# A fused mixer kernel: the second MLP's tokens turned by transposing transfers instead of TensorE

## The chip, the cores and the metric

The kernel runs on one core of one Trainium2 chip, in one launch. The metric is the device time of that core in microseconds: from runs of the whole kernel, the median is given. The trace is of one execution, taken by the hardware profiler; its times are counted from the first instruction.

## The reference

Three layers follow each other over 4 batches of 768 tokens with 384 channels: a gated linear attention with a complex decay, a first MLP behind a low-rank mixing of the tokens, and a second MLP behind a two-dimensional Fourier transform. The change lies in the last, which computes

```python
X = np.fft.fft(x, axis=1)
X = np.fft.fft(X, axis=2)
mixed = np.real(X).astype(np.float32)
u = x + mixed
mu = np.mean(u, axis=-1, keepdims=True)
var = np.mean((u - mu) ** 2, axis=-1, keepdims=True)
un = (u - mu) / np.sqrt(var + 1e-06)
ch = np.maximum(un @ w_ch1, 0.0) @ w_ch2
return (u + ch).astype(np.float32)
```

`w_ch1` is 384 x 1536 and `w_ch2` is 1536 x 384. Products are kept at nearly float32 accuracy: each operand is split into a float16 part and a float16 rest, and three products of the parts are summed.

## The kernel before

The work of a batch is cut in two **groups** of 384 tokens, `(b, g)`. For the second MLP there are eight groups, (0,0) to (3,1). A group takes 12 steps `f`, one for each 128 hidden channels. A step has nine matmuls that make the hidden values (`first_product`, lines 192 to 198 with `mm3`, lines 105 to 107), ScalarE's `hh` (line 201) and VectorE's `hl` (line 204), the two float16 parts of the rectified hidden values, and nine matmuls that add them to three sums (lines 210, 211 and 224).

`first_product` needs the normalised tokens with **channels on partitions**, 384 tokens long, in two float16 parts. The tokens lie with tokens on partitions, so `make_un` (line 1446) normalises three tiles of 128 tokens on VectorE (line 1453, `un`), turns each 128x128 block with TensorE (line 1459, nine for a group, into a PSUM bank `nt`), and splits the bank: ScalarE makes the float16 part (line 1461), VectorE subtracts it from the bank to make the rest (line 1462).

While a group's matmuls run, the next group's tokens are made ready. The generator `moe_units` gives two **slots** a step, numbered `n` = 0 to 47 over the two groups of a batch, and `put` (line 1536) hands the yields of a generator to slots:

```python
put(make_un(b, 1), (16, 17, 18, 19, 21, 23))
...
put(make_un(after, 0), (40, 41, 42, 43, 45, 47))
```

An even slot's work stands ahead of that step's `hh` and `hl`, an odd slot's behind them. Slots of the first group also hold the Fourier transform of the next batch (`dft`, line 1268): its folds on VectorE, its float16 parts `eeh`, `eel`, `ooh`, `ool` (lines 1327 and 1335, in slots 13 and 14), its first products `ac` and `as` on TensorE (slots 15 and 17), the parts and squares of those (lines 1327, 1335, 1341), and behind them the rest, which ends in slot 35 with the factors that `make_un(after, 0)` needs. Slot 40 holds the loads of the batch after that (`dft_loads`, line 1258: five transfers on SP's queue, the gathers on POOL's). The stores of a finished group (line 1469) go out on SP's queue, too.

From the second phase on (line 1517) every engine and queue runs its instructions in the order in which the program names them; `in_order` (line 591) makes each depend on the one before it on its engine. An instruction that waits thus holds back all behind it on its engine.

Tiles come from rings: the ring `un` has four buffers of 1536 bytes a partition, used by `un` and by the folds of `dft`; a PSUM ring of three banks (`ms`) holds `nt`, `ac`, `as` and the later products of `dft`. A tile waits until all readers of the ring's buffer four (or three) tiles earlier are done. `raw_cc` and `raw_ss` hold the Fourier constants until they are split, in slots 15 to 18 of the last group of the first MLP, and are unused from then on.

Of the kernel before, what the change touches and what calls it, by code (L numbers as in the profile page):

```python
# [8 lines left out]
F16 = mybir.dt.float16  # L9
# [7 lines left out]
ALU = mybir.AluOpType  # L17
# [5 lines left out]
DM = H * D  # L23
# [20 lines left out]
def whole_of(ap):  # L44
    return ap if ap.dtype == F16 else f32(ap)
# [3 lines left out]
def mixer_kernel(ctx, tc, a_in, qk_in, v_in, u_in, v4_in, w_in, cc_in, ss_in, cb_in, sb_in, id_in, mask_in, rows_in, out):  # L49
    nc = tc.nc  # L50
    V, A, G, T = nc.vector, nc.scalar, nc.gpsimd, nc.tensor
# [12 lines left out]
    def bank(name, pool=None):  # L64
        pool = pool or pms
        return pool.tile([128, 512], F32, tag={id(pms): "ms", id(pacc): "acc", id(phid): "hid"}[id(pool)], name=name)
# [9 lines left out]
    def pair(name):  # L76
        if parts16[0]:
            return moe.tile([128, 2, 384], F16, tag="u", name=name, bufs=5)
        return pfl[0].tile([128, 2, 384], F32R, tag="u32", name=name, bufs=3)
# [65 lines left out]
    parts16 = [True]  # L145
# [29 lines left out]
    def check_w(mi, f, z):  # L175

        hi = wt[mi, f][:, 0, z * 384 : (z + 1) * 384]
        unread = ft(f"chk{mi}_{f}_{z}", [128, 384], BF16, tag="chk", bufs=1)
        at = stats[:, list(BOUNDS).index(("w1", "w2")[z]), mi * FB + f : mi * FB + f + 1]
        kept(V.scalar_tensor_tensor, out=unread, in0=hi, scalar=1.0, in1=hi, op0=ALU.mult, op1=ALU.mult, accum_out=at)  # L180
# [35 lines left out]
    def moe_units(todo):  # L216

        acc = {}
        late = []
        lows = []  # L220

        def low(mi, b, g, f, hl, t):
            last_step = f == FB - 1
            T.matmul(acc[t], hl[:, TSS[t]], wt[mi, f][:, 0, 384:], start=False, stop=last_step and mi == 1)  # L224
            if last_step:
                if mi == 0:
                    extra1(b, g, t, acc[t])
                (finish1, finish2)[mi](b, g, t, acc[t])

        def second(mi, b, g, f, hh, hl, very_last):  # L230
            if f == 0:
                acc.update(enumerate(sums(f"acc{mi}_{b}_{g}")))
            lows.append((mi, b, g, f, hl))
            if very_last:
                for args in lows[:-1]:
                    for t in range(3):
                        low(*args, t)
                del lows[:-1]
            for t in range(3):
                second_product(mi, f, acc, hh, t)  # L240
                if very_last:
                    low(*lows[0], t)
            while not very_last and len(lows) > (f < FB - 1 and parts16[0]):
                args = lows.pop(0)
                for t in range(3):
                    low(*args, t)

        for mi, b in todo:
            for g in range(2):
                for f in range(FB):  # L250
                    hp = first_product(mi, f, (uts, unT)[mi][b, g], f"hp{mi}_{b}_{g}_{f}")
                    yield mi, b, g, f, 0
                    hh, hl = (hidden(f"{x}{mi}_{b}_{g}_{f}", x) for x in ("hh", "hl"))
                    positive(hp, hh)
                    positive_low(hp, hh, hl)
                    yield mi, b, g, f, 1
                    for args in late:
                        second(*args, False)
                    late = [(mi, b, g, f, hh, hl)]
        second(*late[0], True)  # L260
# [163 lines left out]
    def make_ut(b, g):  # L424

        uts[b, g] = pieces = []

        def piece(k):
            xp = bank(f"xp{b}_{g}_{k}")[:, :384]
            tokens(xp, b, g, k)  # L430
            mixed(xp, b, g, k)
            u = pair(f"u{b}_{g}_{k}")
            if parts16[0]:
                A.activation(u[:, 0], xp, AF.Copy, scale=UP)
                V.scalar_tensor_tensor(out=u[:, 1], in0=xp, scalar=UP, in1=u[:, 0], op0=ALU.mult, op1=ALU.subtract)
            else:
                A.copy(u[:, 0], xp)
                V.tensor_tensor(u[:, 1], xp, f32(u[:, 0]), ALU.subtract)
            pieces.append(u)

        for k in range(3):
            piece(k)
            if k == 2 and g == 1 and parts16[0]:
                A.activation(zst[b], f32(zst[b]), AF.Copy, scale=UP * WP[0] * WP[1])
            yield
# [745 lines left out]
    u2 = {}  # L1191
# [3 lines left out]
    def ft(name, shape, dt=F32, tag=None, bufs=1):  # L1195
        return pfl[0].tile(list(shape), dt, tag=tag or name.split(".")[0], name=name.replace(".", "_"), bufs=bufs)
# [61 lines left out]
    def dft_loads(b):  # L1258
        lo, hi = ([ft(f"{x}.{b}_{i}", [128, DM], tag="lh", bufs=15 if parts16[0] else 6) for i in range(3)] for x in ("lo", "hi"))
        u2[b] = lo, hi  # L1260
        xs[b] = {}
        for i in range(3):
            nc.sync.dma_start(lo[i], x1d[b][i * 128 : (i + 1) * 128, :])
            G.indirect_dma_start(hi[i], None, x1d[b], bass.IndirectOffsetOnAxis(ap=fc["rows"][:, i : i + 1], axis=0))
            if i < (2 if parts16[0] else 1):
                xs[b][i] = others(b, i)
# [179 lines left out]
    def make_un(b, g):  # L1446

        mv, rs = rstd[b]
        unT[b, g] = pieces = []
        uns = []  # L1450
        for t in range(3):
            un = ft(f"un.{b}_{g}_{t}", [128, DM], tag="un", bufs=4 if parts16[0] else 3)
            V.tensor_scalar(un, u2[b][g][t], mv[:, 3 * g + t, 0:1], rs[:, 3 * g + t : 3 * g + t + 1], ALU.subtract, ALU.mult)
            uns.append(un)
            yield
        for k in range(3):
            ps = bank(f"nt{b}_{g}_{k}")[:, :384]
            for t in range(3):
                T.transpose(ps[:, t * 128 : (t + 1) * 128], uns[t][:, k * 128 : (k + 1) * 128], ident)
            u = pair(f"n{b}_{g}_{k}")  # L1460
            A.copy(u[:, 0], ps)
            V.tensor_tensor(u[:, 1], ps, whole_of(u[:, 0]), ALU.subtract)
            pieces.append(u)
            yield
# [36 lines left out]
    def verdict():  # L1501

        tests = [(i, test) for i, x in enumerate(BOUNDS.values()) for test in x]
        ok = ft("ok", [128, len(tests), B * NC], tag="un", bufs=4)
        for o, (i, (op, bound)) in enumerate(tests):
            V.tensor_scalar(ok[:, o], stats[:, i], bound, None, op)
        within = const("within", [128, 1])
        V.tensor_reduce(within, ok, mybir.AxisListType.XY, ALU.add)
        ps = bank("kept")[:1, :1]
        T.matmul(ps, within, one, start=True, stop=True)  # L1510
        broken = const("broken", [1, 1], I32)
        V.tensor_scalar(broken, ps, 128 * len(tests) * B * NC - 0.5, None, ALU.is_lt)
        return broken
# [16 lines left out]
    for mi, b, g, f, half in moe_units([(0, B - 1)] + [(1, b) for b in range(B)]):  # L1530
        n = 2 * (FB * g + f) + half
        if n == 0:
            after = b + 1 if mi else 0
            side = {}

            def put(gen, slots):
                for at in slots:
                    side.setdefault(at, []).append(lambda: next(gen, None))

            if mi == 0:  # L1540
                put((fn() for fn in conversions), (1, 1, 2, 2, 15, 16, 17, 18))
                put(dft(0), FIRST_STEPS)
                put(make_ut(b, 1), (19, 21, 23))
                put(make_un(0, 0), (41, 42, 43, 43, 45, 47))
            else:
                if after < B:
                    put(dft(after), STEPS)
                put(make_un(b, 1), (16, 17, 18, 19, 21, 23))
                if after < B:
                    put(make_un(after, 0), (40, 41, 42, 43, 45, 47))  # L1550
            if after + 1 < B:
                put((dft_loads(x) for x in [after + 1]), [40])
        for item in side.get(n, []):
            item()
        if mi and (b < 2 and n in (24, 36, 44, 46) or b == B - 1 and n < 40):
            check_w(*checks.pop(0))
        if (mi, b, n) == (1, B - 1, 42):
            broken = verdict()
# [207 lines left out]
```

## Time and profile before

| | |
|---|---|
| median of 3 runs | 864.04 us (861.32 to 870.68) |
| the profiled execution | 863.16 us, its span 861.4 us |
| second MLP's first matmul | at 544.1 us |
| PE busy over the span | 93% |
| DVE, ACT busy | 73%, 52% |
| granted TensorE clock | 0.997 of full speed |

Engines: PE is TensorE's matmuls, PEld its weight loads, DVE is VectorE, ACT ScalarE, SP the queue of the plain transfers. Matmuls are pipelined: each is listed with about 0.33 us, but they start some 0.16 us apart, so the time that one takes from its engine is read from the starts.

### The profile page before, as it was taken

The numbers are of one execution on the slowest core, as the hardware profiler recorded it, in microseconds if no ns is written. First come the engines' busy times: TensorE is split into PE (matmuls) and PEld (weight loads), VectorE is DVE, ScalarE is ACT, GpSimd is POOL, SyncE is SP. The second block draws the span as 40 slices with busy tenths as digits, with TensorE's granted clock in tenths as the row PEclk, the third lists the DMA queues.
The fourth block names the chain that finished last, engine by engine and source line by source line (L and its number), as shares of the span: only waits on it lengthen the run. The fifth ranks groups of instructions, "written<-read, shape, count | busy, mean of one in ns | idle before, by whom it ended". The sixth has DMA issues, their size and how long they took to land.

```text
span 861.4 us, 17279 instructions
## 1 busy us (share of the span) xinstructions
PE 799.0 (93%) x6947; PEld 542.1 (63%) x6947; DVE 627.7 (73%) x1304; ACT 450.6 (52%) x845; POOL 36.1 (4%) x79
## 2 busy tenths in 40 slices
PE   0298999999899999999999999999999999999996
PEld 0187755567766677666776665666666666666663
DVE  6989689998779977988965846657485657645652
ACT  7976598798868679758733342142224123311210
POOL 1001000010000000000003200001010100000000
PEclk9999999999999999999999999999999999999999
DMA  9539933588392594359386120103010300000000
GB/s 357 68 67 127 299 108 95 136 160 197 71 200 89 140 201 112 120 125 187 84 133 222 47 74 1 38 1 102 1 47 1 101 29 1 29 1 28 1 29 32
DMA packets 47353, 83.06 MB, mean 96 GB/s; under 512 B 5600, under 2 KB 36576, under 8 KB 47264
## 3 DMA queue, kind: packets, MB, share of 16 engines
q1 hardware_dynamic: 45984, 77.94, 37.6%
q0 software_dynamic: 1280, 3.93, 1.4%
q8 instruction: 56, 0.92, 0.5%
q14 instruction: 33, 0.27, 0.1%
HBM read 53.39 MB, written 9.44 MB: 73 GB/s over the span
## 4 chain that ended last, share of the span: by engine, by line
PE 75%; ACT 12%; DVE 6%; DMA 4%; issue 2%; SPq 1%; DVEq 0%; ACTq 0%
PE acc L210 10%; PE acc L211 10%; PE hp L105 10%; PE hp L107 10%; PE hp L106 10%; PE acc L224 7%; PE sc L325 4%; PE y L343 3%; PE acc L1083 3%; DMA QT<-QK 3%; ACT ain L101 2%; ACT L97 2%; PE g L343 1%; ACT hh L201 1%; PE z L385 1%
## 5 line engine op out<-in xcount | busy, mean ns | idle before, releaser
L201 ACT ACTIVATE hh<-hp 128x384 f16<-128x384 f32 x192 | 93.5, 489 | 303.5 <-PE hp L107 295.3
L204 DVE SCALAR_TENSOR_TENSOR hl<-hp,hh 128x384 f16<-128x384 f32 x192 | 105.6, 554 | 134.5 <-ACT hh L201 133.7
L210 PE MATMUL acc<-w,hh 128*128 128x384 f16 x576 | 187.7, 326 | 3.6 <-ACT hh L201 3.4
L211 PE MATMUL acc<-w,hh 128*128 128x384 f16 x576 | 187.3, 326 | 0.0
L105 PE MATMUL hp<-u,w 128*128 128x384 f16 x288 | 94.6, 328 | 0.1
L107 PE MATMUL hp<-u,w 128*128 128x384 f16 x288 | 94.5, 328 | 0.0
L106 PE MATMUL hp<-u,w 128*128 128x384 f16 x288 | 94.5, 328 | 0.0
L105 PE MATMUL hp<-n,w 128*128 128x384 f16 x288 | 93.9, 326 | 0.0
L107 PE MATMUL hp<-n,w 128*128 128x384 f16 x288 | 93.9, 326 | 0.0
L106 PE MATMUL hp<-n,w 128*128 128x384 f16 x288 | 93.9, 326 | 0.0
L210 PEld LDWEIGHTS <-hh 128*128 128x128 f16 x576 | 56.3, 98 | 40.4 <-ACT hh L201 6.6
L105 PEld LDWEIGHTS <-w 128*128 128x128 f16 x576 | 56.5, 98 | 37.8 <-issue 0.5
L107 PEld LDWEIGHTS <-w 128*128 128x128 f16 x576 | 56.5, 98 | 37.6 <-issue 0.5
L106 PEld LDWEIGHTS <-w 128*128 128x128 f16 x576 | 56.5, 98 | 36.8 <-issue 0.7
L224 PE MATMUL acc<-w,hl 128*128 128x384 f16 x360 | 77.5, 326 | 0.0
L211 PEld LDWEIGHTS <-hh 128*128 128x128 f16 x576 | 56.4, 98 | 33.1 <-issue 0.4
L325 PE MATMUL sc<-QT 96*128 96x128 f32 x384 | 50.0, 284 | 10.6 <-DMA QT<-QK 9.8
L325 PEld LDWEIGHTS sc<-QT 96*128 96x128 f32 x384 | 47.1, 197 | 13.0 <-issue 11.7
L332 PE MATMUL kp<-ident,QK 128*128 128x128 f32 x120 | 19.8, 292 | 33.6 <-DVE QK L309 31.3
L224 PEld LDWEIGHTS <-hl 128*128 128x128 f16 x360 | 35.2, 98 | 23.6
L1083 PE MATMUL acc<-w,hl 128*128 128x384 f16 x216 | 48.6, 327 | 1.4 <-DVE hl L204 1.4
L97 ACT ACT_TABLE_LOAD x33 | 42.3, 1283 | 1.3 <-PEq L1752 0.7
(264 smaller groups left out, 1414.4 us busy)
## 6 DMA issues: line engine op xcount, KB each, us to landing
QT<-QK SPq DMA_DIRECT2D x144, 129.0 KB, 6.9
stw<-in_w_dram SPq DMA_DIRECT2D x48, 384.0 KB, 5.3
ain<-in_a_dram SPq DMA_DIRECT2D x12, 768.0 KB, 7.0
qkin<-in_qk_dram SPq DMA_DIRECT2D x12, 768.0 KB, 6.9
x1d<-x SPq DMA_DIRECT2D x24, 192.0 KB, 3.4
vin<-in_v_dram SPq DMA_DIRECT2D x18, 192.0 KB, 3.4
lo<-x1d SPq DMA_DIRECT2D x12, 192.0 KB, 3.7
out_dram<-lo SPq DMA_DIRECT2D x12, 192.0 KB, 2.0
```

The source lines that it names most:

```text
L97: ordered(lambda: A.preload_act_table_set(name))
L105: T.matmul(o, ah, bh, start=start, stop=False, skip_group_check=skip)
L106: T.matmul(o, ah, bl, start=False, stop=False, skip_group_check=skip)
L107: T.matmul(o, al, bh, start=False, stop=stop, skip_group_check=skip)
L201: A.activation(hh, hp, AF.Relu)
L204: V.scalar_tensor_tensor(out=hl, in0=hp, scalar=0.0, in1=whole_of(hh), op0=ALU.max, op1=ALU.subtract)
L210: T.matmul(acc[t], hh[:, TSS[t]], w[:, 0, 384:], start=f == 0, stop=False)
L211: T.matmul(acc[t], hh[:, TSS[t]], w[:, 1, 384:], start=False, stop=False)
L224: T.matmul(acc[t], hl[:, TSS[t]], wt[mi, f][:, 0, 384:], start=False, stop=last_step and mi == 1)
L325: T.matmul(ps[:, h, :], q[:, 128:256], q[:, :128], start=True, stop=True)
L343: T.matmul(out[p, hsl], l(h)[:, p], r[:, hsl], start=h == 0 and o + done == 0, stop=h == 7 and o + rest == len(ops) - 1, skip_group_check= ...
L1083: T.matmul(accs[t], hls[n][:, TSS[t]], wt[0, every[n][2]][:, 0, 384:], start=False, stop=False)
```

## The change

For the seven groups other than (0,0), in the main path, `make_un` splits first and turns afterwards. Each of its three tiles of 128 tokens is normalised as before (`un`). Then ScalarE writes its float16 part and VectorE the rest into a tile `n16` with tokens on partitions, both now from SBUF, and **one transfer with a transpose**, issued on SP's queue, turns the whole tile of 128 x 768 float16 values into its place in `nt`, a tile with channels on partitions. `nt` lies in the buffers `raw_cc` (groups `g` = 0) and `raw_ss` (`g` = 1). `n16` shares the ring `un`. The nine transposes on TensorE and the three PSUM banks of a group go away. The six yields are given to other slots: 11 to 16 instead of 16 to 23, and 36 to 41 instead of 40 to 47. A yield of an odd place normalises, the next one splits and issues the transfer, in the order of the list.

```diff
         mv, rs = rstd[b]
         unT[b, g] = pieces = []
+        if parts16[0] and (b, g) != (0, 0):
+            nt = ft(f"nt.{b}_{g}", [128, 2, 3, 384], F16, tag=("raw_cc", "raw_ss")[g])
+            pieces.extend(nt[:, :, k] for k in range(3))
+            for t in range(3):
+                un = ft(f"un.{b}_{g}_{t}", [128, DM], tag="un", bufs=4)
+                V.tensor_scalar(un, u2[b][g][t], mv[:, 3 * g + t, 0:1], rs[:, 3 * g + t : 3 * g + t + 1], ALU.subtract, ALU.mult)
+                yield
+                n = ft(f"n16.{b}_{g}_{t}", [128, 2, DM], F16, tag="un", bufs=4)
+                A.copy(n[:, 0], un)
+                V.tensor_tensor(n[:, 1], un, n[:, 0], ALU.subtract)
+                to = nt.rearrange("d z k t -> d (z k) t")[:, :, t * 128 : (t + 1) * 128]
+                nc.sync.dma_start_transpose(out=to, in_=n.rearrange("t z d -> t (z d)"))
+                yield
+            return
         uns = []
...
-                put(make_un(b, 1), (16, 17, 18, 19, 21, 23))
+                put(make_un(b, 1), (11, 12, 13, 14, 15, 16))
                 if after < B:
-                    put(make_un(after, 0), (40, 41, 42, 43, 45, 47))
+                    put(make_un(after, 0), (36, 37, 38, 39, 40, 41))
```

## Rows read from the trace of the kernel before

**Rows 1.** The page: span; busy us, share of the span and instructions of each engine.

```profile
span 861.4 us, 17279 instructions
...
PE 799.0 (93%) x6947; PEld 542.1 (63%) x6947; DVE 627.7 (73%) x1304; ACT 450.6 (52%) x845; POOL 36.1 (4%) x79
```

**Rows 2.** Busy time by stretch: start:end, length, then each engine; PEclk, DMA share, GB/s.

```profile
544.10:861.40 317.30, 309.61 (x2079) 195.75 (x2077) 188.21 (x524) 79.65 (x183) 9.26 (x11) 1.00 0.09 30
586.80:623.50 36.70, 36.70 (x240) 22.76 (x238) 21.92 (x64) 7.43 (x17) 2.99 (x4) 1.00 0.19 60
623.50:665.70 42.20, 41.88 (x305) 27.60 (x304) 27.36 (x70) 14.82 (x35) 2.16 (x2) 1.00 0.08 24
```

**Rows 3.** Waits of TensorE from 544 us on: us in total, times, longest.

```profile
PE nt L1459 <- ACT as L1341: 0.8, 3, 0.3
```

**Rows 4.** Line 1459 from 544 us on: count, duration min/median/max, first and last start.

```profile
L1459 PE MATMUL nt<-ident,un x63: 272/273/329, 576.6 to 815.7; 128*128 128x128 f32 x63
```

**Rows 5.** TensorE in order of time: start, us, instruction and count (seven places).

```profile
610.79 0.33 PE L105 MATMUL hp<-n,w 128*128 128x384 f16 x1
...
613.71 0.33 PE L105 MATMUL hp<-n,w 128*128 128x384 f16 x1
...
615.18 0.49 PE L1459 MATMUL nt<-ident,un 128*128 128x128 f32 x3
615.50 0.33 PE L210 MATMUL acc<-w,hh 128*128 128x384 f16 x1
...
623.47 0.33 PE L105 MATMUL hp<-n,w 128*128 128x384 f16 x1
...
646.58 0.24 PE L107 MATMUL as<-ss,ool 128*97 128x192 f16 x1
...
665.69 0.33 PE L105 MATMUL hp<-n,w 128*128 128x384 f16 x1
...
817.25 0.33 PE L105 MATMUL hp<-n,w 128*128 128x384 f16 x1
```

**Rows 6.** Groups by line and shape, from 380 us on: count, busy us, mean ns, idle before.

```profile
L1462 DVE TENSOR_TENSOR n<-nt,n 128x384 f16<-128x384 f32 x24 | 13.1, 547 | 4.1 <-ACT n L1461 4.1
...
L1461 ACT CAST n<-nt 128x384 f16<-128x384 f32 x24 | 11.4, 474 | 4.3 <-PE nt L1459 4.3
...
L1279 DVE TENSOR_TENSOR xe<-lo,hi 128x384 f32<-128x384 f32 x8 | 4.3, 542 | 0.0
...
L1327 ACT ACTIVATE ooh<-oo 128x776 f16<-128x776 f32 x4 | 3.4, 843 | 0.0
```

**Rows 7.** VectorE in order of time, [idle before <-releaser] (two places).

```profile
612.97 0.56 DVE L204 SCALAR_TENSOR_TENSOR hl<-hp,hh 128x384 f16<-128x384 f32 x1 [1.98 <-ACT hh L201]
...
643.21 0.56 DVE L204 SCALAR_TENSOR_TENSOR hl<-hp,hh 128x384 f16<-128x384 f32 x1 [0.22 <-ACT hh L201]
643.95 0.97 DVE L1335 SCALAR_TENSOR_TENSOR eel<-ee,eeh 128x776 f16<-128x776 f32 x1 [0.18 <-ACT eeh L1327]
644.83 0.96 DVE L1335 SCALAR_TENSOR_TENSOR ool<-oo,ooh 128x776 f16<-128x776 f32 x1
```

**Rows 8.** ScalarE in order of time.

```profile
650.54 0.49 ACT L201 ACTIVATE hh<-hp 128x384 f16<-128x384 f32 x1 [2.23 <-PE hp L107]
```

**Rows 9.** Transfers, whole span: a queue's packets, MB, share; issues, KB each, us to landing.

```profile
q1 hardware_dynamic: 45984, 77.94, 37.6%
...
QT<-QK SPq DMA_DIRECT2D x144, 129.0 KB, 6.9
...
lo<-x1d SPq DMA_DIRECT2D x12, 192.0 KB, 3.7
out_dram<-lo SPq DMA_DIRECT2D x12, 192.0 KB, 2.0
```

**Rows 10.** SP's queue in order of time: start, us in issuing, line, count.

```profile
592.62 0.45 SPq L1263 DMA_DIRECT2D lo<-x1d  x1
...
594.61 0.38 SPq L1263 DMA_DIRECT2D lo<-x1d  x1
```

**Rows 11.** Line 318, QT<-QK: its landing times.

```profile
DMA to landing us min/median/max: 3.1/6.9/9.6
```

## The prediction, made before the changed kernel was run

> **What bounds the kernel now.** I read the page first: TensorE is busy 93% of the span [rows 1]. An average over two phases says little, so next the busy time by stretch. In the second MLP TensorE works 309.61 of 317.30 us, at a granted clock of 1.00; in a group without a Fourier transform beside it 36.70 of 36.70 us, in one with it 41.88 of 42.20, while VectorE has 21.92 and 27.36 us of work there, ScalarE 7.43 and 14.82 [rows 2]. The reader is to see that nothing but TensorE's own work sets the length of this phase. The list of TensorE's waits agrees: from 544 us on one kind is left, 0.8 us in three waits, and it is a transpose that waits [rows 3]. So a microsecond taken off TensorE there is a microsecond off the end, and one that another engine adds counts only where TensorE then has to wait.
>
> **What goes.** 63 transposes stand after 544 us, all of them in the seven groups changed [rows 4]. Their listed 273 ns is the length of one in the pipeline, not its price. That is read from the starts: three transposes begin at 615.18, the next matmul at 615.50, 0.32 to 0.33 us for three [rows 5]. 21 such triples are 6.9 us. With them goes the wait of 0.8 us [rows 3], since no `nt` asks for a PSUM bank. The most that can be won is 7.7 us: there is no other idle time of TensorE in these groups, and its clock is full.
>
> **What is exchanged.** A group has three casts and three subtractions before and after. From PSUM they take 474 and 547 ns; the nearest rows from SBUF are 542 ns for a VectorE operation of this size, and 843 ns for a ScalarE cast of twice the size, so about 0.42 to 0.47 us for ours [rows 6]. I take no difference; a gain of a few hundredths each would fall in idle time. The three `un` stay.
>
> **What is moved.** Ahead of group (b+1,0), slots 36 to 41, both engines are mostly idle (VectorE waits 1.98 us ahead of one `hl` [rows 7]): nothing. Ahead of (b,1), slots 11 to 16, the work now stands among the last folds and the splits of `dft`. Ahead of `ool` in VectorE's order come two `un` and one subtraction, at starts 0.47 us apart 1.41 us (`eel` and `ool` start 0.88 us apart at 0.97 each [rows 7], so 0.09 overlaps: 0.55 takes 0.46 to 0.47). VectorE's idle time there, 0.22 + 0.18 us, takes up part [rows 7]. `ool` ended at 645.79; TensorE first reads it at 646.58 [rows 5, 7]: 0.79 us of slack. 1.41 - 0.40 - 0.79 = 0.22 us late, in three groups (b = 0, 1, 2): 0.7 us. If no idle time can be used it is 0.62 us each, 1.9 in all; if the engine overlaps more, nothing. I take 0.7.
>
> **What is added: 21 transposing transfers** of 192 KB. The trace has none. From below, a plain transfer of that size lands in 2.0 us (stores) to 3.7 us (loads); the nearest row that goes from SBUF to SBUF on the same queue, `QT<-QK`, 129 KB a transfer by the profile's count, has a median of 6.9 us and at most 9.6 in a stretch where the queue is crowded [rows 9, 11]. Cut in rows of 128 values (256 bytes) a transfer has 768 packets; the queue's mean packet cost 37.6% x 16 x 861.4 / 45,984 = 0.113 us for a mean of 1.7 KB, so by packets 768 x 0.113 / 16 = 5.4 us at most, and by bytes (77.94 MB in 37.6% of 861.4 us is 241 GB/s) 0.8 us. In this phase the queue is nearly empty (DMA share 0.09 [rows 2]), so I go by the bytes and the quiet 192 KB rows: 1 to 3 us of the queue, 2 to 5 us to landing, with no gain to be had below that, since the bytes have to move.
>
> What hides them: a step takes 613.71 - 610.79 = 2.92 us [rows 5]. Ahead of (1,0) the split of tile 2 stands behind the `hl` at 612.97, and both take 0.47 us from start to start [rows 7]; so the three transfers go out near 608.1, 611.1 and 614.0. The first product that reads them was at 623.47 and comes 1.0 us earlier without the three triples [rows 5]: 8.5 us of cover for the last. Ahead of (1,1) it is longer: tile 0's split stands ahead of the `hl` at 643.21 and, with one `un` and one subtraction more, its transfer goes out near 644.0, the last near 650; the reader, at 665.69 before, comes 1.3 us earlier (the triples and a wait), at 664.4 [rows 3, 5, 7]. Ahead of (3,1), without a transform, the first goes out six steps ahead of the reader: the reader at 817.25 - 1.0 = 816.2, the transfer at 798.7 [rows 5]. Three things are queued. **On SP's queue** the five loads of slot 40 stand between the second and the third transfer. Before, they went out from 592.62 on, long ahead of their slot, since nothing held them [rows 10]; now they wait for tile 1's split, to 611. Their readers are the folds of the next batch, after 623.5, and the batch takes 594.61 + 3.7 - 592.62 = 5.7 us, so they land by 617. The third transfer then stands behind them, and lands by 619 to 622. In time, with 0.5 us or more to spare. Stores wait for nothing new. **POOL's queue** is not moved past. **In the ring `un`** the third `n16` takes the first one's buffer, so ScalarE's third cast waits until the first transfer has landed, and `hh` and the square of `ac` stand behind it. That square frees the bank of the next `as`; ScalarE had 2.23 us idle ahead of that `hh` at 650.54, and the square stands right behind it [rows 8]. With a cast of 0.47 the first transfer may land as late as 650.1: 6.1 us after it was issued. At 2 to 5 us nothing is lost.
>
> **Sum:** 6.9 + 0.8 - 0.7 = 7.0 us off the profiled execution's 863.16 gives 856.2. That execution stands 0.9 us below the median of the runs; on the median, 864.04 - 7.0 = **857.0**.
>
> On the price of a turned block the Trainium skill has two figures. "VectorE: DVE Perf Modes", section "The three transpose paths", gives 1309 ns for a 128x128 block by the DMA crossbar, and the rules of that page advise TensorE wherever PSUM can take the result, which speaks against this change; six such blocks one after the other are, as an estimate, 7.9 us a transfer, and the sum would be about 900 us. "DMA: Bandwidth & Descriptors", section "Latency and other measured facts", gives 261 GB/s, as an estimate 0.75 us, which leaves the sum as it is. No row of this trace tells which holds.
>
> **The rivals.**
> *Crowding:* VectorE and ScalarE run late ahead of (b,1), and TensorE waits for `eel`, `ool` or for a bank. For it: VectorE is almost without gaps there, and a wait of 0.2 us is already forecast. Against: ScalarE is free, and later slots are emptier by the work moved out of them. If each of the three groups loses 1 to 2 us, the gain is 7.7 - 3 to 7.7 - 6: 859 to 862, say 860.5.
> *Slower:* the transfers run one after the other on SP's queue, each as long as the nearest SBUF-to-SBUF row, 6.9 us. They would land at 608.1 + 20.7 = 628.8 against a reader at 622.5: TensorE stands 6.3 us, ahead of (1,0), (2,0) and (3,0), 18.9 us. Ahead of (3,1), with no transform beside it, 798.7 + 20.7 against 816.2: 3.2 us. Ahead of the other (b,1) only the wait in the ring counts, 644.0 + 6.9 against 650.1: 0.8 us, three times. 24.5 us against 7.0 won: about 881. At 9.6 us each the same working gives 14.4 x 3 + 11.3 + 8.4 x 3 = 80 us, 937. It decides from (622.5 - 608.1) / 3 = 4.8 us a transfer on. For it: the nearest row, and that the values are turned. Against: that row is from a crowded stretch, and 241 GB/s by bytes. The skill's 1309 ns belongs to this rival.
> *The edit does less than it says:* if TensorE's starts close up by less than the triples' 0.33 us, because another wait fills it, there is no change, 864. TensorE without gaps on both sides of each triple speaks against it.
>
> **How the numbers follow.** The forecast has a chance of 0.63 (its own range 854 to 860, by the runs' scatter and the 0.7 us), crowding 0.12, the slow transfers 0.21, no effect 0.04. A measurement of this kernel tells about 1% from no change, 8.6 us: faster is below 855.4, slower above 872.7. Even the full 7.7 us stays short of that, so faster by over 1% comes only from the scatter of the runs (861.32 to 870.68): 0.17. Within 1% takes the rest of the forecast, crowding and no effect: 0.61. Slower 0.22. The range 853.5 to 882 leaves out the far half of the slow transfers, and a little scatter below.
>
> **What would show it.** Right: from 544 us on no transpose on TensorE; groups of 35.6 us without a transform and some 41 us with one; the transfers landing in under 5 us; no wait of TensorE for `nt`; `as` with waits of a few tenths. Wrong: a wait of the first product of a group for a transfer; ScalarE's cast waiting for one ahead of `hh`; loads that land behind the folds; or TensorE waits for `eel` and `ool` of over 0.6 us a group.

## The result, and the profile after

The changed kernel takes **856.0 us** (median of 14 runs, 854.33 to 859.34) against 863.87 us (14 runs): ratio 0.9906, 95% interval 0.9884 to 0.9929. Forecast were 857.0 us and a ratio within 1% of no change, on the faster side. Two single executions, 1698 us with the kernel before and 2124 us with all eight groups turned by transfers, are far off the rest: the medians below hold them, the ratios leave them out.

The head of the page and its line on DMA packets, changed kernel, and behind them the same line of the kernel before:

```profile
span 853.8 us, 17228 instructions
...
PE 791.8 (93%) x6884; PEld 534.8 (63%) x6884; DVE 627.7 (74%) x1304; ACT 451.1 (53%) x845; POOL 36.0 (4%) x79
...
DMA packets 64153, 87.19 MB, mean 102 GB/s; under 512 B 22400, under 2 KB 53376, under 8 KB 64064
...
DMA packets 47353, 83.06 MB, mean 96 GB/s; under 512 B 5600, under 2 KB 36576, under 8 KB 47264
```

TensorE has 63 instructions less than in [rows 1], VectorE and ScalarE as many as before. Now the busy time by stretch: the whole second MLP, group (0,1) and group (1,0), the stretches of [rows 2]:

```profile
544.80:853.80 309.00, 302.34 (x2017) 188.31 (x2014) 188.04 (x524) 80.19 (x183) 9.26 (x11) 0.99 0.17 44
586.20:621.90 35.70, 35.70 (x231) 21.70 (x229) 21.90 (x64) 7.51 (x17) 3.00 (x4) 1.00 0.31 78
621.90:662.70 40.80, 40.73 (x295) 26.51 (x294) 27.21 (x70) 14.78 (x35) 2.19 (x2) 1.00 0.15 40
```

The second MLP goes from 317.3 to 309.0 us, 8.3 less. The span falls by 7.6 only, since this execution's first phase, which the change does not touch, was 0.7 us longer. Groups without a transform fall by 1.0 us, those with one by 1.4, and TensorE is as full as before.

TensorE's waits from 535 us on, in place of [rows 3]:

```profile
PE nt L1473 <- DVE un L1467: 1.4, 1, 1.4
```

That one belongs to group (0,0), which is turned as before. No first product waits for a transfer. The transfers by their line: SP's time in issuing (min/median/max, first and last start), and the times to landing:

```profile
L1461 SPq DMA_TRANSPOSE nt<-n x21: 1210/1222/2057, 565.7 to 799.7; - x21
...
DMA to landing us min/median/max: 2.7/2.7/2.8
```

This trace holds the landing of six of the 21 transfers, none of them behind other transfers on the queue. A second trace of the same kernel (the changed kernel run again, below) holds all 21:

```profile
DMA to landing us min/median/max: 2.7/2.7/4.6
```

There 18 land in 2.7 to 2.9 us and one in 3.5; the two that stand behind five loads, ahead of (1,0) and (2,0), land in 4.6 and 3.6 us. Packets under 512 bytes rose from 5600 to 22,400, 800 a transfer: 768 rows of 256 bytes (128 float16 values) make up its 192 KB; what the other 32 are is not shown. SP's queue ahead of (1,0), where the loads stand between the second and third transfer (start, us in issuing):

```profile
607.61 4.14 SPq L1461 DMA_TRANSPOSE nt<-n  x2
611.79 0.57 SPq L1263 DMA_DIRECT2D lo<-x1d  x1
...
613.83 0.43 SPq L1263 DMA_DIRECT2D lo<-x1d  x1
614.36 1.22 SPq L1461 DMA_TRANSPOSE nt<-n  x1
```

The third goes out at 614.36 and its reader begins at 621.9. In the second trace it goes out at 623.6, lands at 628.2, and its reader begins at 631.1: 2.9 us to spare.

### The profile page after: what moved, and what is told of

Same layout as the page of the kernel before. It is cut to its first block, busy times and chain, and to the rows that moved or that the text cites. A ratio compares the mean times of both kernels' runs of the same rounds, so it can differ in the third digit from the quotient of the medians.

```text
span 853.8 us, 17228 instructions
## 1 busy us (share of the span) xinstructions
PE 791.8 (93%) x6884; PEld 534.8 (63%) x6884; DVE 627.7 (74%) x1304; ACT 451.1 (53%) x845; POOL 36.0 (4%) x79
## 2 busy tenths in 40 slices
DMA packets 64153, 87.19 MB, mean 102 GB/s; under 512 B 22400, under 2 KB 53376, under 8 KB 64064
## 4 chain that ended last, share of the span: by engine, by line
PE 74%; ACT 10%; DMA 6%; DVE 6%; SPq 2%; issue 1%; DVEq 0%; ACTq 0%
PE acc L210 10%; PE acc L211 10%; PE hp L105 10%; PE hp L107 10%; PE hp L106 10%; PE acc L224 7%; PE sc L325 4%; PE y L343 3%; DMA QT<-QK 3%; PE acc L1083 3%; ACT ain L101 2%; ACT L97 2%; PE g L343 2%; PE warm L609 1%; PE kp L332 1%
## 5 line engine op out<-in xcount | busy, mean ns | idle before, releaser
L105 PE MATMUL hp<-nt,w 128*128 128x384 f16 x252 | 82.2, 326 | 0.0
L106 PE MATMUL hp<-nt,w 128*128 128x384 f16 x252 | 82.2, 326 | 0.0
L107 PE MATMUL hp<-nt,w 128*128 128x384 f16 x252 | 82.2, 326 | 0.0
L325 PEld LDWEIGHTS sc<-QT 96*128 96x128 f32 x384 | 47.1, 197 | 12.8 <-issue 11.6
```

The lines of the kernel that those rows point to most:

```text
L105: T.matmul(o, ah, bh, start=start, stop=False, skip_group_check=skip)
L106: T.matmul(o, ah, bl, start=False, stop=False, skip_group_check=skip)
L107: T.matmul(o, al, bh, start=False, stop=stop, skip_group_check=skip)
L325: T.matmul(ps[:, h, :], q[:, 128:256], q[:, :128], start=True, stop=True)
```

## The experiments

Nine runs, each beside runs of the kernel before on the same chip. The first phase varies from execution to execution, by several microseconds (its end lies between 541 and 554 us in the profiles below, with the same instructions up to its last group), so each run is also judged by the length of its second MLP, from its first product to the end of the span, which repeats to 0.2 us (309.0 and 308.9 in two traces of the changed kernel, 309.1 and 308.9 in two with all eight groups).

**The slots alone.** The transposes stay on TensorE; the pieces lie in the two constant buffers.

```diff
+        nt = ft(..., [128, 2, 3, 384], F16, tag=("raw_cc", "raw_ss")[g]) if ... (b, g) != (0, 0) else None
-            u = pair(f"n{b}_{g}_{k}")
+            u = pair(f"n{b}_{g}_{k}") if nt is None else nt[:, :, k]
-                put(make_un(b, 1), (16, 17, 18, 19, 21, 23))
+                put(make_un(b, 1), (11, 12, 13, 14, 15, 16))
-                    put(make_un(after, 0), (40, 41, 42, 43, 45, 47))
+                    put(make_un(after, 0), (36, 37, 38, 39, 40, 41))
```

> The kernel before with the moved slots alone: TensorE still turns the blocks, the pieces lie in the two unused constant buffers, as in the change (the old ring of five can't hold a third piece that early). My theory: the time is TensorE's own work, so no change but for the 0.8 us of waits for a bank: ratio to before 0.998 to 1.003 (862 to 866 us), with 63 transposes at 0.33 us a triple still there. Rival: a part of the 8 us comes from the earlier slots and the other buffers, then 856 to 861 us (ratio 0.991 to 0.997).

Measured: 867.59 us, ratio 1.0064 (1.0042 to 1.0086): slower than either theory said. Its second MLP and TensorE's waits there:

```profile
541.80:861.30 319.50, 309.18 (x2079) 195.42 (x2077) 188.09 (x524) 79.26 (x183) 9.26 (x11) 0.99 0.09 30
```

```profile
PE ac L105 <- DVE nt L1463: 3.5, 3, 1.2
```

2.2 us longer than before: the 0.8 us of waits ahead of `nt` are gone, but in the three groups with a transform `ac` now asks for a bank of the ring that `nt` still holds, and waits up to 1.2 us. The early slots win nothing by themselves. The medians differ by 5.3 us (867.59 against 862.25 beside it). The other 3 us are not in this trace, whose execution took 863.06 us and whose first phase, 541.8 us, is no longer than the 544.1 before; where the other executions lost them is not shown.

**Each transpose twice.**

```diff
-            for t in range(3):
+            for t in [*range(3)] * (1 if (b, g) == (0, 0) else 2):
                 T.transpose(ps[:, t * 128 : (t + 1) * 128], uns[t][:, k * 128 : (k + 1) * 128], ident)
```

> The kernel before with each of the 63 transposes done twice into the same bank, nothing else changed. My theory: a triple costs 0.33 us of a TensorE without gaps, so 21 more triples cost 6.9 us: 870.8 us, ratio 1.008 (1.006 to 1.010). Rival: a transpose's listed 273 ns is its price, then 17 us more (ratio 1.020); or part of it hides in waits, then under 4 us (ratio below 1.005).

Measured: 872.04 us, ratio 1.0095 (1.0065 to 1.0126), and in the trace:

```profile
548.30:872.60 324.30, 316.49 (x2143) 202.69 (x2140) 189.36 (x524) 80.87 (x183) 9.23 (x11) 0.99 0.09 29
```

324.3 - 317.3 = 7.0 us for 21 more triples, 0.33 us each, with no new wait. This is the price of the transposes, shown by itself: the starts give it, the listed duration does not.

**The transfers at the old slots.**

```diff
-                put(make_un(b, 1), (11, 12, 13, 14, 15, 16))
+                put(make_un(b, 1), (16, 17, 18, 19, 21, 23))
-                    put(make_un(after, 0), (36, 37, 38, 39, 40, 41))
+                    put(make_un(after, 0), (40, 41, 42, 43, 45, 47))
```

> The changed kernel with the slots of before (16 to 23 and 40 to 47): the last transfer of a group goes out next to its reader. My theory: it lands 2.7 us after its issue, and the splits stand behind the last hl (and, ahead of (1,1), (2,1), (3,1), behind the sums of the transform), so the first product waits about 5 us ahead of (1,1) and (2,1) and (0,1), and 2 to 3 us ahead of (1,0), (2,0), (3,0), (3,1): 20 to 26 us over the changed kernel, 876 to 882 us, slower than before (ratio 1.014 to 1.021). Rival: the transfers are so short that their place does not matter, then 856 to 860 us.

Measured: 891.06 us, ratio 1.0336 (1.0306 to 1.0366). TensorE's waits from 530 us on, and the first of them by stretch (the wait, then three pieces of what follows):

```profile
PE hp L105 <- DMA nt<-n: 24.7, 7, 4.2
```

```profile
586.40:590.60 4.20, 0.04 (x1) 0.00 (x0) 2.31 (x9) 0.00 (x0) 0.00 (x0) 0.96 0.24 47
590.70:592.00 1.30, 1.30 (x5) 0.61 (x6) 0.00 (x0) 0.00 (x0) 0.00 (x0) 0.50 0.00 0
592.00:593.00 1.00, 1.00 (x5) 0.47 (x4) 0.00 (x0) 0.00 (x0) 0.00 (x0) 0.50 0.00 0
593.50:596.00 2.50, 2.50 (x25) 1.78 (x24) 1.69 (x6) 0.71 (x2) 0.00 (x0) 0.96 0.00 0
```

The waits are 24.7 us, as expected. But the second MLP takes 343.3 us, 34.3 more than in the changed kernel:

```profile
544.90:888.20 343.30, 311.56 (x2016) 191.19 (x2014) 188.42 (x524) 79.73 (x183) 9.13 (x11) 0.97 0.15 40
```

After the first wait the granted clock is 0.50, the 1.2 GHz level: matmuls start 0.32 us apart instead of 0.16.

```profile
590.64 0.48 PE L105 MATMUL hp<-nt,w 128*128 128x384 f16 x1 [4.20 <-DMA nt<-n]
590.92 0.52 PE L106 MATMUL hp<-nt,w 128*128 128x384 f16 x1
591.24 0.52 PE L107 MATMUL hp<-nt,w 128*128 128x384 f16 x1
```

So a late transfer can cost its lateness and more: 9.6 us went beside the 24.7, which I had left out, and 9.2 of them are TensorE's busy time grown for the same matmuls (311.56 against 302.34 us). Not every wait did this. Over the 5 us behind each of the seven, the mean granted clock was 0.66 to 0.69 five times and 1.00 twice, behind 3.05 us ahead of (2,0) and 2.94 us ahead of (3,1). Two waits of nearly the same length, 3.02 us ahead of (3,0) and 3.05 ahead of (2,0), show both:

```profile
804.00:809.00 5.00, 4.98 (x21) 2.61 (x22) 1.05 (x4) 0.49 (x1) 0.00 (x0) 0.66 0.00 0
718.30:723.30 5.00, 4.99 (x31) 3.04 (x32) 2.75 (x6) 0.49 (x1) 0.00 (x0) 1.00 0.02 5
```

No run separates what makes the difference.

**All eight groups by transfers**, run twice.

```diff
-        if parts16[0] and (b, g) != (0, 0):
+        if parts16[0]:
...
-                put(make_un(0, 0), (41, 42, 43, 43, 45, 47))
+                put(make_un(0, 0), (41, 41, 42, 43, 43, 44))
```

The buffer `raw_cc` is free by then: in the trace of the kernel before its constants are split by 487.4 us, in the group ahead of the last group of the first MLP, which begins at 503.7, and not in that last group.

> The changed kernel with the first group (0,0) turned by transfers too, its yields in slots 41, 41, 42, 43, 43, 44 of the last group of the first MLP. My theory: three triples (1.0 us) and TensorE's wait of 1.4 us for the third un go away, and the last transfer goes out some 5 us ahead of its reader and lands in 2.7: 2 to 2.4 us faster than the changed kernel, about 853.7 us, ratio to before 0.988. Rival: the first group has too little cover, TensorE waits 1 to 3 us for the transfer, and nothing is won (856 to 858).

Measured: 854.61 us, ratio 0.9895 (0.9867 to 0.9923). Against 0.9906 for the change that is too close to tell, so both were run again beside each other.

> The changed kernel itself, beside the next run on the same chip, so that the two can be compared directly. Theory: ratio to before 0.9906 as measured (0.988 to 0.993), no wait of TensorE for nt from a transfer. Rival for the small size: scatter of the first phase, then a ratio outside 0.988 to 0.993.

> All eight groups turned by transfers (the kernel of the run with the first group, again), beside the changed kernel. Theory: the last group of the first MLP is 2.6 us shorter (37.7 instead of 40.3), so 2 to 3 us faster than the changed kernel: ratio to before 0.986 to 0.989, with the second MLP at 309 us as in the changed kernel. Rival: within scatter of the changed kernel (0.990 to 0.992).

Measured: the changed kernel 856.86 us, ratio 0.9903 (0.9871 to 0.9936); all eight 853.61 us, ratio 0.987 (0.9831 to 0.9908). The intervals overlap, so the medians alone do not tell the two apart; the traces do. The last group of the first MLP and the second MLP, first in the changed kernel, then with all eight:

```profile
513.80:554.10 40.30, 38.90 (x272) 24.34 (x271) 22.97 (x64) 10.84 (x26) 0.00 (x0) 1.00 0.12 40
554.10:863.00 308.90, 302.31 (x2016) 188.11 (x2014) 188.00 (x524) 80.17 (x183) 9.26 (x11) 0.99 0.17 44
```

```profile
503.00:540.70 37.70, 37.70 (x263) 23.28 (x262) 23.07 (x64) 11.04 (x26) 0.00 (x0) 1.00 0.22 58
540.70:849.60 308.90, 302.30 (x2016) 188.08 (x2014) 187.99 (x524) 80.18 (x183) 9.13 (x11) 0.99 0.17 44
```

The group is 2.6 us shorter (three triples, 1.0, and the wait, 1.4, make up most of it), the second MLP the same. The first run of this kernel has the group at 37.7 us too, and every other trace here has it at 40.3. The rest of the difference between the two spans, 863.0 and 849.6, lies ahead of this group, where the two kernels are the same. This is the fastest version found; it beats the change by 2.6 us in this group and by 3 us in the medians.

**One block a transfer**, six transfers for one.

```diff
-                nc.sync.dma_start_transpose(out=to, in_=n.rearrange("t z d -> t (z d)"))
+                x = n.rearrange("t z d -> t (z d)")
+                for i in range(6):
+                    nc.sync.dma_start_transpose(out=to[:, i], in_=x[:, i * 128 : (i + 1) * 128])
```

> The changed kernel with each transfer cut into its six 128x128 blocks, six transfers for one, the same bytes. In the changed kernel a transfer occupies SP for 1.22 us and lands 2.7 us after its issue; a plain one occupies it 0.43. My theory: the 1.22 us is 0.4 fixed and the rest by blocks, so a block alone takes about 0.54 us of SP and 18 take 9.7 us; ahead of (1,0) and (2,0), with the five loads between, the last lands at the reader, and the kernel is 0 to 3 us over the changed one (856 to 859 us). Rival: nearly all of the 1.22 us is fixed, then 18 x 1.2 = 21.6 us a group, the last lands 6 to 9 us behind its reader ahead of three groups and 2 to 6 ahead of the others, and the kernel is 25 to 60 us slower, the half clock after each wait included.

Measured: 903.19 us, ratio 1.0498 (1.0436 to 1.056). My theory fell, the rival held. The transfers by their line, and TensorE's waits:

```profile
L1463 SPq DMA_TRANSPOSE nt<-n x126: 1100/1230/2090, 563.2 to 853.8; - x126
...
DMA to landing us min/median/max: 2.3/2.3/3.6
```

```profile
PE hp L106 <- DMA nt<-n: 17.7, 14, 3.6
PE hp L105 <- DMA nt<-n: 16.3, 3, 6.6
```

A block alone occupies SP for 1.23 us, six in one transfer for 1.22: the time is the transfer's, not the block's. Eighteen take 22 us of SP and can't keep up. 34.0 us of waits, and 356.2 - 309.0 = 47.2 us more in the second MLP:

```profile
543.40:899.60 356.20, 313.98 (x2016) 189.70 (x2014) 188.41 (x524) 80.28 (x183) 9.00 (x11) 0.95 0.14 38
```

Of the other 13.2 us, 11.6 are TensorE's busy time grown for the same matmuls (313.98 against 302.34), at a mean granted clock of 0.95: again the lower clock behind waits. Another 0.7 is a wait for VectorE.

**Four slots later.**

```diff
-                put(make_un(b, 1), (11, 12, 13, 14, 15, 16))
+                put(make_un(b, 1), (15, 16, 17, 18, 19, 20))
-                    put(make_un(after, 0), (36, 37, 38, 39, 40, 41))
+                    put(make_un(after, 0), (40, 41, 42, 43, 44, 45))
```

> The changed kernel with all its slots four later (15 to 20 and 40 to 45): two steps, 5.85 us, off the cover. My theory: the last transfer ahead of (1,0), (2,0), (3,0) goes out about 2.8 us ahead of its reader and lands in 2.7, so it is just in time: waits of TensorE for nt of under 1 us in all, and 855 to 858 us. Rival: the cover was needed (other traffic, late splits), then waits of 1 us and more a group and over 862 us.

Measured: 854.89 us, ratio 0.9907 (0.9873 to 0.994).

```profile
PE hp L105 <- DMA nt<-n: 0.5, 3, 0.2
```

```profile
611.72 7.12 SPq L1461 DMA_TRANSPOSE nt<-n  x3
...
543.10:853.20 310.10, 302.84 (x2017) 188.09 (x2014) 188.61 (x524) 79.70 (x183) 9.29 (x11) 0.99 0.16 44
```

Three waits of 0.2 us: ahead of (1,0) the last transfer goes out at 617.6, 2.9 us ahead of its reader at 620.5, and the cover is used up. The second MLP is 1.1 us longer than in the changed kernel, 0.5 of it in these waits. The edit changes one thing more: slot 40, which holds the five loads, is now that of the first yield and no longer of the fifth, so the loads go out ahead of all three transfers (from 590.3 on) and not between them. In the changed kernel the third transfer ahead of (1,0) has 7.5 us of cover and lands 4.6 us behind its issue in the second trace, so 2.9 us are to spare there, and not 5.85.

**Each transfer twice.**

```diff
-                nc.sync.dma_start_transpose(out=to, in_=n.rearrange("t z d -> t (z d)"))
+                for _ in range(2):
+                    nc.sync.dma_start_transpose(out=to, in_=n.rearrange("t z d -> t (z d)"))
```

> The changed kernel with each transfer issued twice, the second behind the first's landing, since it writes the same place. My theory: transfers cost nothing as long as the last lands ahead of its reader. A tile then takes SP about 5 us; ahead of (1,0) and (2,0), with the loads between, the last lands some 2 us late, elsewhere in time: 2 to 6 us over the changed kernel, 858 to 862 us, all of it in TensorE's waits for nt. Rival: transfers cost by themselves (ports, queue, ScalarE held in the ring), then 21 x 2.7 = 57 us more.

Measured: 864.99 us, ratio 1.0019 (1.0 to 1.0038), over the expected 858 to 862.

```profile
PE hp L105 <- issue: 6.3, 2, 3.3
```

Who waited for the transfers, in the view of their line:

```profile
  PE hp L105: 6.3, 2
```

The second MLP:

```profile
547.80:866.70 318.90, 305.67 (x2017) 189.09 (x2014) 188.13 (x524) 80.27 (x183) 9.21 (x11) 0.98 0.23 56
```

Only the two groups named wait, (1,0) and (2,0), where the last transfers go out behind the loads; the list of TensorE's waits names no releaser ("issue"), the view of the transfers' line does. The second MLP is 9.9 us longer: 6.3 of waits (I had some 2 each, they are 3.1 and 3.3) and 3.6 behind them, where the clock falls again and TensorE's busy time grows by 3.3 (305.67 against 302.34); I had expected all of it in the waits. For the other five groups TensorE waits for no doubled transfer. Three of the stretches in which these run are as long as in the changed kernel to 0.05 us; the other two begin with the lower clock and are 1.3 and 1.7 us longer. So the rival's 57 us are out.

## Why the prediction was right, step by step

**What goes** was right in mechanism and size: 0.33 us a triple, shown alone by the doubling, 6.9 us; the waits for a bank, counted with 0.8 us, are gone and were worth 1.1 (below).

**Crowding** was sized too high, 0.7 us where nothing was lost. VectorE ahead of (1,1), changed kernel, and TensorE's first read of `ool`:

```profile
642.50 0.96 DVE L1335 SCALAR_TENSOR_TENSOR eel<-ee,eeh 128x776 f16<-128x776 f32 x1
643.37 0.48 DVE L1455 TENSOR_SCALAR un<-hi,mv,rs 128x384 f32<-128x384 f32 x1
643.76 0.96 DVE L1335 SCALAR_TENSOR_TENSOR ool<-oo,ooh 128x776 f16<-128x776 f32 x1
...
645.11 0.55 DVE L204 SCALAR_TENSOR_TENSOR hl<-hp,hh 128x384 f16<-128x384 f32 x1
```

```profile
644.97 0.24 PE L107 MATMUL as<-ss,ool 128*97 128x192 f16 x1
```

`ool` ends at 644.72, 0.25 us ahead of its reader; before, 0.79 ahead [rows 5, 7]. The slack shrank by 0.54 us and not by 1.01: a `un` takes 0.39 us from start to start, not 0.47, so 1.25 us were added and not 1.41, and 0.71 us of them fell in gaps that I had read as 0.40. The prices were read from start to start and the gaps from end to start, and the two do not add up. Before, ahead of `hl` and of `eel`:

```profile
642.37 0.35 DVE L1295 TENSOR_TENSOR ee<-g 128x194 f32<-128x194 f32 x1
642.64 0.35 DVE L1296 TENSOR_TENSOR oo<-g 128x194 f32<-128x194 f32 x1
643.21 0.56 DVE L204 SCALAR_TENSOR_TENSOR hl<-hp,hh 128x384 f16<-128x384 f32 x1 [0.22 <-ACT hh L201]
```

These small operations start 0.27 us apart, `hl` starts 0.57 behind the last of them, and `eel` 0.74 behind `hl`, whose price is 0.47: by starts the gaps are 0.30 and 0.27, 0.57 of the 0.71.

That term accounts for 0.7 of the 1.3 us by which the second MLP beat the forecast (8.3 against 7.0). The other 0.6 shows where steps are compared one by one, from first product to first product. Of the 21 steps that lost a triple, 18 are 0.33 to 0.34 us shorter. The three in which the triple had to wait are 0.70 shorter, where 0.33 + 0.27 were counted: the wait, too, was read from end to start, and that is 0.3 in all. One such step, in group (1,0), before and then after (4.61 and 3.90 us from these rounded starts):

```profile
657.28 0.33 PE L105 MATMUL hp<-n,w 128*128 128x384 f16 x1
...
661.89 0.33 PE L105 MATMUL hp<-n,w 128*128 128x384 f16 x1
```

```profile
655.35 0.33 PE L105 MATMUL hp<-nt,w 128*128 128x384 f16 x1
...
659.25 0.33 PE L105 MATMUL hp<-nt,w 128*128 128x384 f16 x1
```

Another 0.2 lies behind the start of TensorE's last matmul (7.0 us to the end of the span before, 6.8 after), where nothing was changed, and 0.1 is spread over the other steps. So the 7.7 us that I called the most that can be won were 0.6 too few.

**What is exchanged:** a cast from SBUF takes 505 ns, more than the 474 from PSUM, where I had 420 to 470; a subtraction 550 against 547. Both lie in idle time, as said:

```profile
L1459 DVE TENSOR_TENSOR n<-un,n 128x384 f16<-128x384 f32 x21 | 11.6, 550 | 0.4
L1458 ACT CAST n<-un 128x384 f16<-128x384 f32 x21 | 10.6, 505 | 11.3 <-DVE un L1455 11.3
```

**The transfers** were taken at 2 to 5 us and land in 2.7, nearer to the stores' 2.0 than to `QT<-QK`'s 6.9 [rows 9], and in 4.6 and 3.6 behind the loads. The choice by bytes and quiet rows held, but no row of the trace before could have decided it: it was a judgement, with 0.21 left to the slow rival. The cover of 8.5 us for the last transfer was worked out rightly where no loads stand between: ahead of (3,0) it is 8.4 (766.4 to 774.8). Ahead of (1,0) it is 7.5, since the loads take 2.5 us of SP; there the transfer has 2.9 us to spare, where 0.5 or more was forecast. The slow rival's mechanism, TensorE held up by late transfers, is real: with 1.23 us of SP a block the kernel is 5% slower. It did not decide because one transfer carries six blocks. Its prices left out the lower clock that followed most of such waits.

**The figures of the Trainium skill.** The 1309 ns a block ("VectorE: DVE Perf Modes", section "The three transpose paths") lie near the 1.23 us that a transfer of one block holds SP here (whether they are the same thing no run shows), but they don't add up by blocks: six in one take 1.22. The estimate of 7.9 us a transfer is refuted by the trace; the other, 0.75 us, is shorter than the 2.7 to landing, but the sum is the same by both. The page's advice (section "Rules for kernel authors"), TensorE where PSUM can take the result, does not hold here, where TensorE has no gap (35.70 of 35.70 us in group (0,1)); for a TensorE with gaps no run here speaks.

What the change needs is both of its parts: slots alone, ratio 1.0064; transfers at the old slots, 1.0336; together 0.9906. The early slots cost because `nt` holds banks there, and without `nt` they are free; the transfers cost because they are late, and with early slots they are not.

## What to carry to other kernels

Where one engine has no gaps, an operation on it is worth the distance between starts, not its listed duration, and its gain can be counted from the trace before anything is built: 6.9 us here. Work moved to a queue is free as long as its last piece lands ahead of its reader: count issue time, landing and everything that stands between on the queue, and put many blocks into one transfer. A wait of a few microseconds on TensorE can cost more than its length: behind five of the seven waits of 2.9 to 4.2 us with the old slots, TensorE ran at half clock for a while. And in one sum read prices and gaps the same way, both from start to start.

## What was not expected

A transfer with a transpose holds SP for 1.22 us, whether it turns one block of 128x128 (1.23) or six, where a plain one of 192 KB holds it 0.43; it lands in 2.3 us with one block (median of the 14 landings that the trace holds), in 2.7 with six, and in 3.6 and 4.6 behind five loads. After TensorE's wait of 4.2 us for a transfer the granted clock was 0.50 for the next first product (590.7 to 593.0), and was back at 0.96 on average from 593.5 to 596.0; after two of the other six waits it did not fall.
